# An adaLN block with segment-memory attention: the opening rearranged (modulation on TensorE, key and query blocks interleaved, weight splits in another place)

## The chip, the cores and the metric

The kernel runs on one core of one Trainium2 chip. The metric is the time of one execution on the device in microseconds; a kernel's time is the median of several runs. A profile is one execution, recorded by the hardware profiler; its times count from the start of the span.

## What is computed

One sequence of 2048 rows of 512 values (`x`) passes through an attention with a compressive memory and then through a gated bilinear network. A conditioning vector `c` gives six vectors of 512 (shift, scale and gate for each half) through one matrix. Cut to what matters here:

```python
mod = (silu(c) @ w_mod).reshape(1, 6, 1, 512)
sa, ca, ga, sb, cb, gb = (mod[:, i] for i in range(6))

h = layernorm(x) * (1 + ca) + sa
q, k, v = h @ wq, h @ wk, h @ wv          # 32 heads of 16, 4 segments of 512 rows
for s in range(4):
    p = softmax(q_s k_s^T / 4 + causal)
    a_mem = (phi(q_s) M) / (phi(q_s) z + 1e-6)     # phi(t) = t + 1 if t > 0 else exp(t)
    o_s = g * a_mem + (1 - g) * (p v_s)            # g = sigmoid(beta), per head
    M, z = M + phi(k_s)^T v_s, z + sum(phi(k_s))
x = x + ga * (o @ wo)
h = layernorm(x) * (1 + cb) + sb
x = x + gb * (((h @ w_gate) * (h @ w_up)) @ w_down)
```

Everything is float32. The projections are done as three products of split operands: each operand is written as a high part, rounded for TensorE's fast float32 form, and a low part, the rest; high times high, low times high and high times low are added up.

## The kernel before, in words

**Stages.** The sequence is cut into four segments of 512 rows, and the heads into four groups of eight. For one segment the normalised rows are transposed into four tiles of 128 columns (`h`, split into `ahH` and `ahL`), and each group's keys and queries come from twelve matmuls per block (`a_kq`: four column tiles, three products each). Keys and queries are written to DRAM in three bfloat16 parts (`kd`, `qd`) and read back in another layout (`kst`, `qst`) by `load`. Then a loop over 32 units (a segment, a group, half of its heads) does the scores twice: once for the row maxima (`q_step`, tiles `q`, reduced on VectorE into `nm`), once for the exponentials (`k_step`, tiles `k` and `pt`), and then the product with the values (`av_step`, tile `tb`). What the next segments need (projections, layer norm, memory) is fed in between as filling. The last part of the program is the network (`acc`, `X`, `Y`, `Z`).

**The opening**, which is where the change is, runs ahead of that loop, for segment 0. Its parts are:

- the silu of `c` (`s_c`), and the gates from `beta` (`gg`, `omg`, `hmg` and one column of each value tile `v`)
- 20 warm-up matmuls on zeros (`warm`, tile `wups`) while the first loads are under way
- the modulation for the first layer norm, in two halves of 256 columns of shift and scale each (`mod0(0)`, `mod0(1)`, weights `wm`, result `m`, then `mod0_out` into `modc`). The first half is 16 one-column products on TensorE with warm-up matmuls between; the second is summed on VectorE, scaled by `s_c`, and reduced by TensorE with a column of ones
- the layer norm `ln`: statistics, reciprocal root, normalising four tiles of `x`, 16 transposes into four banks (`atp`, one bank for each column tile), and for each column tile shift and scale on ScalarE (`ahf`), high part and low part on VectorE
- the weight splits: `load_g(nm, w, g)` loads the keys' or queries' weights of one group (`wrk`, `wrq`), makes the high part on ScalarE (`wkH`, `wqH`) and the low part on VectorE or GpSimd (`wkL`, `wqL`). `load_v` does the same for the value weights
- `a_kq(0, 0, ...)`, `a_v(0)` (tile `vps`), `a_kq(0, 1, ...)`, with parts of the scores of unit 0 between.

**What sets the order.** TensorE's order is written out: every matmul and transpose is chained to the one before by the helpers `MM` and `TP` (lines 85 and 88). `CV` and `CA` are such chains for VectorE and ScalarE (both record line 39), so what is called through them stays in the order of the program. What is called through `vec`, `act` or `nc.gpsimd` is placed by a scheduler that has its own model of times, within the data's dependences; `pin` only ties a place to TensorE's last instruction. All loads and stores here are issued from SP's queue, in the order that the scheduler gave them. The buffers of the raw weights are taken from a list of tags (`stage`), so that group 1's and group 2's raw weights lie where the four tiles of `x` lay, and their loads wait until these are transposed. The gating of the chip's TensorE clock is outside of the program; the profile tells it as a granted share.

The driver of the opening in the kernel before reads, in short:

```python
next(lng); next(lng)      # statistics, normalising
mod0(0)
next(lng); next(lng)      # column tiles 0 and 1
mod0(1)
hcur[0] = run(lng)        # column tiles 2 and 3
```

## Time and profile before

| | us |
|---|---|
| median of 3 runs | 870.56 |
| lowest and highest | 870.12, 871.88 |
| the profiled execution | 869.22 |
| its span | 867.5 |
| TensorE busy in the span | 840.5 |
| VectorE busy | 649.4 |
| ScalarE busy | 495.9 |
| GpSimd busy | 276.3 |

Busy times of engines overlap, so they don't add up to the span. The granted TensorE clock has a mean of 0.998 over the span. A row of a timeline gives start, length (of the whole run, where several alike are merged), engine, line, operation, output and inputs, shape, and in brackets the idle time just before it with what ended it. The pages call the weight load PEld and the matmul PE; a float32 product is two instructions of each. A matmul's length includes its way through the array, and the next one starts before it ends, so the cost of one in a row is the distance of the starts.

### The profile page before, as it was taken

The page shows a single profiled execution, that of the slowest core. Times are in us where ns is not written, and L with a number is a line of the kernel's source. Part 1 is how long each engine was busy: PE and PEld are TensorE (multiplying, and loading weights), DVE is VectorE, ACT ScalarE, POOL GpSimd, SP SyncE. Part 2 cuts the span into 40 slices and gives each one's busy share as a digit, 9 for nine tenths or more (in the row PEclk, how much of TensorE's full clock was granted, in tenths as well). Part 3 has the DMA queues.
Part 4 walks back from the last instruction along what each step waited for, and adds up shares of the span by engine and source line. Part 5 has one row for each costly group of instructions (what it writes and reads, how often), then busy time and mean ns, then how long its engine had stood idle before and what let it go on. Part 6 is the DMA issues. An engine that isn't in the chain of part 4 may idle for free.

```text
span 867.5 us, 14401 instructions
## 1 busy us (share of the span) xinstructions
PE 840.5 (97%) x4969; PEld 598.1 (69%) x4970; DVE 649.4 (75%) x1802; ACT 495.9 (57%) x757; POOL 276.3 (32%) x424
## 2 busy tenths in 40 slices
PE   8989999999999999999999999999999999999998
PEld 5755656565665566665666677788888778888886
DVE  8698766887778877778879457989987855446654
ACT  3758757677777686677544626344536546365230
POOL 4545536466546574586424620000000000000000
PEclk9999999999999999999999999999999999999999
DMA  7555443546436444547476348559561575435002
GB/s 235 160 165 133 128 108 102 174 128 178 125 97 178 129 129 134 135 144 235 133 234 181 124 160 269 203 199 339 204 239 49 187 264 213 161 134 182 28 22 97
DMA packets 83928, 139.57 MB, mean 161 GB/s; under 512 B 12720, under 2 KB 46768, under 8 KB 83856
## 3 DMA queue, kind: packets, MB, share of 16 engines
q1 hardware_dynamic: 83568, 138.52, 50.7%
q8 instruction: 39, 0.64, 0.3%
q14 instruction: 33, 0.27, 0.1%
q10 hardware_dynamic: 288, 0.15, 0.1%
HBM read 89.87 MB, written 48.50 MB: 160 GB/s over the span
## 4 chain that ended last, share of the span: by engine, by line
PE 81%; DVE 12%; ACT 5%; issue 1%; DMA 0%; DVEq 0%; ACTq 0%
PE acc L1337 14%; PE tb L85 8%; PE Xu L1268 7%; PE Xg L1268 7%; PE k L85 6%; PE q L85 6%; DVE q L39 6%; PE vps L85 5%; PE wops L85 5%; PE Yu L1268 4%; PE Yg L1268 4%; PE qps L85 3%; PE kps L85 3%; ACT pt L324 2%; PE Zg L1268 1%; PE Zu L1268 1%
## 5 line engine op out<-in xcount | busy, mean ns | idle before, releaser
L39 DVE CUSTOM_DVE_ANT_0 q<-q,cmask 128x384 f32<-128x384 f32 (+3 forms) x512 | 245.7, 508 | 61.0 <-PE q L85 53.1
L324 ACT ACTIVATE pt<-k 128x1024 f32<-128x1024 f32 x160 | 163.9, 1024 | 65.0 <-PE k L85 64.5
L330 POOL TENSOR_SCALAR_AFFINE_SELECT pt<-pt 128x256 f32<-128x256 f32 (+1 forms) x224 | 98.0, 452 | 165.0 <-ACT pt L324 164.6
L85 PE MATMUL q<-kst,qst 96*128 96x384 bf16 (+3 forms) x512 | 103.1, 298 | 12.5 <-DVE nm L39 11.2
L85 PE MATMUL k<-qst,kst 98*128 98x384 bf16 (+3 forms) x512 | 97.1, 302 | 4.4 <-ACT pt L324 4.2
L1345 DVE TENSOR_TENSOR xa<-xa,acc 128x512 f32<-128x512 f32 x95 | 64.7, 683 | 39.9 <-PE acc L1337 39.4
L85 PE MATMUL tb<-pt,v 128*32 128x512 f32 (+3 forms) x1024 | 75.5, 436 | 0.0
L39 DVE DVE_READ_ACCUMULATOR2_ANT nm<- 128x1 f32 x512 | 71.8, 140 | 0.0
L85 PEld LDWEIGHTS <-kst 98*128 98x128 bf16 x512 | 37.7, 98 | 48.8 <-issue 42.8
L85 PEld LDWEIGHTS <-qst 96*128 96x128 bf16 x512 | 45.6, 97 | 34.9 <-issue 12.5
L1337 PE MATMUL acc<-dH,mH 128*128 128x512 f32 (+1 forms) x152 | 60.3, 397 | 0.0
L1337 PE MATMUL acc<-dL,mH 128*128 128x512 f32 (+1 forms) x152 | 60.1, 395 | 0.0
L1337 PE MATMUL acc<-dH,mL 128*128 128x512 f32 (+1 forms) x152 | 60.0, 395 | 0.0
L85 PEld LDWEIGHTS tb<-pt,v 128*32 128x32 f32 x1024 | 28.7, 109 | 38.6 <-issue 34.8
L356 ACT ACTIVATE tsb<-tb 128x512 f32<-128x512 f32 x32 | 19.1, 596 | 40.2 <-PE tb L85 40.2
L1337 PEld LDWEIGHTS acc<-dL,mH 128*128 128x128 f32 (+1 forms) x152 | 28.6, 188 | 7.1
L1337 PEld LDWEIGHTS acc<-dH,mL 128*128 128x128 f32 (+1 forms) x152 | 28.5, 188 | 7.1 <-DVE mL L1288 0.3
L1337 PEld LDWEIGHTS acc<-dH,mH 128*128 128x128 f32 (+1 forms) x152 | 28.5, 188 | 6.7
L85 PE MATMUL kps<-ahH,wkH 128*128 128x512 f32 x64 | 29.9, 466 | 0.0
L85 PE MATMUL wops<-woH,oH 128*128 128x512 f32 x64 | 28.2, 440 | 0.7 <-ACT oH L519 0.7
L85 PE MATMUL qps<-ahH,wqH 128*128 128x512 f32 x64 | 28.7, 448 | 0.0
L85 PE MATMUL vps<-wvH,ahH 128*128 128x512 f32 x64 | 28.3, 442 | 0.0
(400 smaller groups left out, 2031.3 us busy)
## 6 DMA issues: line engine op xcount, KB each, us to landing
wm<-in_w_mod_dram SPq DMA_DIRECT2D x24, 256.0 KB, 4.5
kd<-k SPq DMA_DIRECT2D x16, 384.0 KB, 2.5
kst<-kd SPq DMA_DIRECT2D x32, 192.0 KB, 3.2
qd<-q SPq DMA_DIRECT2D x16, 384.0 KB, 2.8
qst<-qd SPq DMA_DIRECT2D x32, 192.0 KB, 3.6
x<-in_x_dram SPq DMA_DIRECT2D x16, 256.0 KB, 4.5
kst<-kd SPq DMA_DIRECT2D x32, 128.0 KB, 3.1
qst<-qd SPq DMA_DIRECT2D x32, 128.0 KB, 3.5
```

Of the source, the lines that this page charges most:

```text
L39: i = getattr(self.eng, name)(*a, **k)
L85: return pe(nc.tensor.matmul(*a, **k))
L324: ex = act.activation(pt, kp, AF.Exp, scale=0.25)
L330: sels[u, i] = nc.gpsimd.affine_select(w, w, pattern=[[0, w.shape[1]], [1, P]], compare_op=ALU.is_ge, fill=0.0, base=0, channel_multiplier=-1)
L356: act.activation(tsbs[u], tbs.pop(u), AF.Copy)
L1268: pe(nc.tensor.matmul(ps[0:n], a, b[:, k], start=first and c == 0, stop=last and c == 5, skip_group_check=True))
L1337: pe(nc.tensor.matmul(ps, a[0:m, t * P:(t + 1) * P], b[0:m], start=j == 0, stop=j == n - 1))
L1345: vec.tensor_add(xa, xa, ps)
```

## The change

Nothing behind the opening is edited. The order of instructions differs on every engine, up to the first scores on TensorE and to the loads of segment 1's `x` on SP. The core of the diff:

```diff
-            eng.tensor_scalar(b, mv[:, :, 1], 1.0, EPS, op0=ALU.mult, op1=ALU.add)
-            eng.tensor_mul(b, b, a)
+        if first:
+            CV.scalar_tensor_tensor(b, mv[:, :, 1], EPS, a, op0=ALU.add, op1=ALU.mult)
...
+        tps = [bank(f"{pfx}tp{s}_{d}") for d in range(KT)] if first else []
         for t in range(4):
             i = V.tensor_scalar(xt[t], xt[t], mv[:, t, 0:1], y[:, t:t + 1],
...
+            for d, ps in enumerate(tps):
+                TP(ps[:, t * P:(t + 1) * P], xt[t][:, d * P:(d + 1) * P], ident)
...
             if fast:
-                V.tensor_copy(hi, h)
+                if d % 2:
+                    A.activation(hi, h, AF.Copy)
+                else:
+                    V.tensor_copy(hi, h)
                 V.tensor_sub(lo, h, hi.bitcast(F32))
...
-    for a in kst:
-        nc.gpsimd.memset(a[96:98].rearrange("p h t -> p (h t)").bitcast(F32), ONES2)
...
+    scl = CV.tensor_mul(s_c, s_c, e1)
+    for a in kst:
+        tc.add_manual_dep(nc.gpsimd.memset(a[96:98].rearrange("p h t -> p (h t)").bitcast(F32), ONES2).ins, scl.ins.name, SYNC, reason="order")
...
+    def gates():
...
+    MW = 96
...
     def mod0(j):
-        ps = mp0[j][:, 0:4]
-        if j == 0:
+        ps = mp0[j].rearrange("p (i n) -> p i n", n=P)[:, :, 0:MW]
+        for k in range(KT):
             for i in range(4):
-                for k in range(KT):
-                    MM(ps[:, i:i + 1], r0[0][k][:, i * P:(i + 1) * P], s_c[:, k:k + 1],
-                       start=k == 0, stop=k == KT - 1)
-                    if i == 0:
-                        warm(2)
-                if 0 < i < 3:
-                    warm(2)
-            a0 = r0[1][0]
-            CV.tensor_scalar_mul(a0, a0, s_c[:, 0:1])
-            for k in range(1, KT):
-                CV.scalar_tensor_tensor(a0, r0[1][k], s_c[:, k:k + 1], a0, op0=ALU.mult, op1=ALU.add)
...
+                MM(ps[:, i], r0[j][k][:, i * P:(i + 1) * P], s_c[:, k:k + 1].to_broadcast([P, MW]),
+                   start=k == i == 0, stop=k == KT - 1, skip_group_check=True)
...
-        A, V = (CA if g == 0 else act), (CV if g == 0 and nm == "q" else nc.gpsimd)
+        A, V = CA if g < 2 else act, CV if g == 0 else nc.gpsimd
...
+            three = ((wH, hH), (wH, hL), (wL, hH)) if s == 0 and g < 2 else ((wH, hH), (wL, hH), (wH, hL))
+            terms = [(k, *ab) for k in range(KT) for ab in three]
+            if s == 0 and g == 1:
+                terms.sort(key=lambda t: t[1] is wL)
...
-                        i = act.activation(a, f, fn)
+                        i = (CA if fast else act).activation(a, f, fn)
...
-    next(lng)
     mod0(0)
     next(lng)
+    mod0_out(0, mp0[0])
+    mod0(1)
+    next(lw[0])
     next(lng)
-    mod0(1)
-    hcur[0] = run(lng)
+    next(lng)
+    mod0_out(1, mp0[1])
     next(lw[1])
...
     kq0 = [a_kq(0, 0, "k"), a_kq(0, 0, "q")]
+    for kq in kq0:
+        next(kq)
+        next(kq)
+    run(lng)
+    for _ in range(4):
+        next(lw[2])
...
+    gates()
```

`gates()` holds what was written out before at the place of the silu: the two exponentials of `beta`, the sums and reciprocals, the copies into the value tiles and the products into `hmg`. It is called behind the splits of group 1.

What that makes of the order shows at two places. The first is TensorE from the modulation to the first key block. `wm_0` to `wm_3` are the modulation weights of the four row tiles of `w_mod`, `x_0` to `x_3` the four tiles of rows, and `atp_0` to `atp_3` the four column tiles. Before, from the end of the first half on (the second transposes and the key block follow):

```order
L85 MATMUL m_272<-s_c,wm_2_239 128x1
L85 MATMUL m_272<-s_c,wm_3_240 128x1
L88 MATMUL atp_0_366<-ident,x_0_206 128x128
L88 MATMUL atp_0_366<-ident,x_1_208 128x128
L88 MATMUL atp_0_366<-ident,x_2_210 128x128
L88 MATMUL atp_0_366<-ident,x_3_212 128x128
L88 MATMUL atp_1_377<-ident,x_0_206 128x128
L88 MATMUL atp_1_377<-ident,x_1_208 128x128
L88 MATMUL atp_1_377<-ident,x_2_210 128x128
L88 MATMUL atp_1_377<-ident,x_3_212 128x128
L85 MATMUL m_273<-ones,wm_0_237 128x1 x4
L88 MATMUL atp_2_394<-ident,x_0_206 128x128
```

All four transposes of a column tile stand together, eight of them ahead of the second half's reduction and eight behind it. Now, from the end of the last transposes on:

```order
L88 MATMUL atp_2_321<-ident,x_3_208 128x128
L88 MATMUL atp_3_322<-ident,x_3_208 128x128
L85 MATMUL m_251<-s_c,wm_0_233 128x96 x4
L85 MATMUL m_251<-s_c,wm_1_234 128x96 x4
L85 MATMUL m_251<-s_c,wm_2_235 128x96 x4
L85 MATMUL m_251<-s_c,wm_3_236 128x96 x4
L85 MATMUL kps_0_379<-ahH_0_365,wkH_253 128x512
L85 MATMUL kps_0_379<-ahL_0_366,wkH_253 128x512
L85 MATMUL kps_0_379<-ahH_0_365,wkL_254 128x512
```

The second half is done on TensorE as 16 products behind all 16 transposes, which go tile by tile of `x`; the first key and query blocks follow and take turns by column tile (0 and 1 of the keys, 0 and 1 of the queries, then 2 and 3 of each).

The second place is ScalarE from the value weights to the splits of group 1 (`wkH` and `wqH` in the last rows of each). Before:

```order
L39 ACTIVATE wvH_286<-wrv_288 128x512
L39 ACTIVATE wvH_290<-wrv_292 128x512
L39 ACTIVATE kf_0_435<-kps_0_422 128x512
L39 ACTIVATE k_0_0_437<-kf_0_435 128x512
L39 ACTIVATE wvH_294<-wrv_296 128x512
L39 ACTIVATE wvH_298<-wrv_300 128x512
L842 ACTIVATE rlk_0_479<-kf_0_435 128x512
L842 ACTIVATE phk_0_478<-kf_0_435 128x512
L39 ACTIVATE qf_0_469<-qps_0_456 128x512
L39 ACTIVATE q_0_0_471<-qf_0_469 128x512
L761 ACTIVATE wkH_449<-wrk_448 128x4x8x16
L761 ACTIVATE wqH_453<-wrq_452 128x4x8x16
```

Now:

```order
L39 ACTIVATE wvH_272<-wrv_274 128x512
L39 ACTIVATE wvH_276<-wrv_278 128x512
L39 ACTIVATE kf_0_422<-kps_0_379 128x512
L39 ACTIVATE k_0_0_424<-kf_0_422 128x512
L39 ACTIVATE qf_0_442<-qps_0_386 128x512
L39 ACTIVATE q_0_0_444<-qf_0_442 128x512
L39 ACTIVATE rlk_0_452<-kf_0_422 128x512
L39 ACTIVATE phk_0_451<-kf_0_422 128x512
L39 ACTIVATE wkH_432<-wrk_431 128x4x8x16
L39 ACTIVATE wqH_436<-wrq_435 128x4x8x16
L39 ACTIVATE gg<-be 128x32
```

All four value weights stand ahead of the keys' evacuation, the queries' follows the keys' at once, ahead of the features, and the splits of group 1 are chained behind them (line 39 in place of 761). On GpSimd their low parts now stand ahead of the gates' copies, and the low part of group 0's key weights has gone to VectorE, between the two writes of `modc`.

More of the change, by code (lines that the diff above doesn't have):

```diff
@@ L147, in tile_kernel @@
     hm8 = cst.tile([P, HG], F32, name="hm8")
-    vec.tensor_reduce(hm8, ident.rearrange("p (d h) -> p h d", h=HG), axis=AX.X, op=ALU.add)
+    CV.tensor_reduce(hm8, ident.rearrange("p (d h) -> p h d", h=HG), axis=AX.X, op=ALU.add)
     for g in range(NG):
-        vec.tensor_copy(hmg[:, g], hm8.unsqueeze(2).to_broadcast([P, HG, VS]))
+        CV.tensor_copy(hmg[:, g], hm8.unsqueeze(2).to_broadcast([P, HG, VS]))
     modc = cst.tile([P, 16], F32, name="modc")
@@ L206, in ln @@
         hH, hL = [], []
+        if first:
+            hcur[0] = hH, hL
         for d in range(KT):
-            ps = bank(f"{pfx}tp{s}_{d}", small=pfx == "c" and s == 0)
-            for t in range(4):
-                TP(ps[:, t * P:(t + 1) * P], xt[t][:, d * P:(d + 1) * P], ident)
+            if first:
+                ps = tps[d]
+            else:
+                ps = bank(f"{pfx}tp{s}_{d}", small=pfx == "c" and s == 0)
+                for t in range(4):
+                    TP(ps[:, t * P:(t + 1) * P], xt[t][:, d * P:(d + 1) * P], ident)
             h = pool.tile([P, L], F32, tag="hf", name=f"{pfx}hf{s}_{d}", bufs=hb[2])
@@ L846, in feature2 @@
                 def feature2():
-                    pin(vec.scalar_tensor_tensor(e, e, 1.0, rl, op0=ALU.min, op1=ALU.add))
+                    pin((CV if fast else vec).scalar_tensor_tensor(e, e, 1.0, rl, op0=ALU.min, op1=ALU.add))
                 held = s == 0 and g > 1
```

58 lines of the change are left out of this document (25 added, 33 removed).

## The prediction

> **What bounds the kernel now.** I read the page's shares first, then the chain of waits over the first 90 us, then each engine's timeline of that stretch, since the order of the instructions differs nowhere behind about 50 us.
>
> ```profile
> PE 840.5 (97%) x4969; PEld 598.1 (69%) x4970; DVE 649.4 (75%) x1802; ACT 495.9 (57%) x757; POOL 276.3 (32%) x424
> PE 81%; DVE 12%; ACT 5%; issue 1%; DMA 0%; DVEq 0%; ACTq 0%
> ```
>
> TensorE is busy for 97% of the span and holds 81% of the chain that ended last. So an opening that ends earlier brings the rest forward as a block, unless something behind it is tied to another clock. What the opening waits for stands in the chain (start, length, what):
>
> ```profile
> 10.82 1.91 DVE x L39 x4
> 12.74 1.68 DVE wm L39
> ...
> 16.11 0.67 DVE wm L39
> ...
> 16.83 1.20 PE m L85 x8
> 18.02 1.40 PE atp L88 x6
> ...
> 26.51 5.58 PE vps L85 x24
> ...
> 39.76 0.51 PE q L85 x2
> ```
>
> Until 16.8 us VectorE decides: it normalises `x`, then sums the second half of the modulation weights (`wm`) by itself, four passes over 512 columns. TensorE waits for that sum, reduces it (`m`), does the second eight transposes (`atp`), and from there is bound by itself up to the first scores (`q`). TensorE's timeline gives its prices:
>
> ```profile
> 8.79 0.28 PE L85 MATMUL m<-s_c,wm 128*128 128x1 f32 x2
> 13.66 0.95 PE L85 MATMUL m<-s_c,wm 128*128 128x1 f32 x8
> 14.46 1.07 PE L88 MATMUL atp<-ident,x 128*128 128x128 f32 x8
> 16.83 1.20 PE L85 MATMUL m<-ones,wm 128*128 128x1 f32 x8 [1.29 <-DVE wm L39]
> 17.89 1.95 PE L88 MATMUL atp<-ident,x 128*128 128x128 f32 x8
> 26.35 0.39 PE L85 MATMUL vps<-wvH,ahH 128*128 128x512 f32 x1
> 39.68 0.59 PE L85 MATMUL q<-kst,qst 96*128 96x512 bf16 x2
> 50.04 1.09 PE L85 MATMUL mz<-v,pkr 128*128 128x136 f32 x8
> ```
>
> A 512-column matmul of the projections costs 5.58/24 = 0.232 us, by the chain's piece at 26.51. Eight transposes cost (1.07 − 0.27)/7 = 0.114 us each at full clock, their own duration of 0.27 taken off. The second eight need nearly twice that, and the granted clock (second value from the right of the last four) tells why:
>
> ```profile
> 16.00:17.00 1.00, 0.17 (x2) 0.18 (x2) 0.77 (x3) 0.79 (x2) 0.00 (x0) 1.00 1.02 377
> 17.00:18.00 1.00, 1.00 (x9) 1.00 (x10) 0.94 (x2) 0.66 (x1) 0.00 (x0) 0.79 0.16 57
> 20.00:21.00 1.00, 1.00 (x4) 0.75 (x3) 0.67 (x2) 1.00 (x3) 0.00 (x0) 0.50 0.40 118
> 21.00:22.00 1.00, 1.00 (x6) 0.82 (x5) 0.97 (x3) 1.00 (x2) 0.00 (x0) 1.00 1.10 332
> ```
>
> The clock falls to 0.50 at about 17.6 us, after the 1.29 us wait, and is back at 21.0. So the wait costs twice: itself, and half the speed for 3.4 us.
>
> **The change part by part.** *Modulation on TensorE.* Removed: four VectorE passes, eight one-column reductions, twelve warm-up matmuls among the first half's products. Added: both halves as 16 products each, 96 columns wide, which are 32 instructions a half (two per float32 product, as in the x2 and x8 of the rows). No row shows this shape. Below stands the one-column product, 0.114 us (0.95 less a duration of 0.15 or so, over 7); above, if load and product did not overlap, the 0.23 of 512 columns. The nearest row is `mz`, float32 with 136 columns: (1.09 − 0.28)/7 = 0.116. I take 0.116, so 3.71 us a half. TensorE comes free for the first at 8.79 as before. Its line is then:
>
> - first half 8.79 + 3.71 = 12.50
> - sixteen transposes × 0.114 = 1.83, to 14.33
> - second half 3.71, to 18.04
> - 24 matmuls of the first key and query blocks × 0.232 = 5.57, to 23.61.
>
> The values' matmuls begin at 23.61 where they began at 26.35: 2.74 us earlier, provided that nothing else is late. Each supplier in turn:
>
> The data of the second half: its last load is issued by 8.56 us and lands at most 6.2 later, at 14.8; its product is due at 14.33 + 2.78 = 17.1.
>
> ```profile
> 6.12 2.44 SPq L654 DMA_DIRECT2D wm<-in_w_mod_dram  x4
> DMA to landing us min/median/max: 5.0/5.9/6.2
> ```
>
> The normalised `x`: even at its old time (10.82, done at 12.73) the four tiles arrive at 11.3, 11.8, 12.3 and 12.73, and transposes that take one tile after the other ask for them at 12.50, 12.96, 13.4 and 13.9. So the layer norm's shorter arithmetic, the gates moved behind and the memsets of `kst` moved behind the silu gain nothing by themselves. The memsets could cost:
>
> ```profile
> 1.77 3.97 POOL L248 MEMSET kst<- 2x1024 f32 x4
> 7.60 1.49 POOL L672 TENSOR_TENSOR hmg<-hmg,gg 128x128 f32<-128x128 f32 x4
> 29.10 1.94 POOL L762 TENSOR_TENSOR wkL<-wrk,wkH 128x512 fp32r<-128x512 f32 x1 [14.98 <-ACT wkH L761]
> 30.98 2.12 POOL L762 TENSOR_TENSOR wqL<-wrq,wqH 128x512 fp32r<-128x512 f32 x1
> ```
>
> VectorE's and ScalarE's prices, for this and for what follows, are
>
> ```profile
> 8.44 0.66 DVE L39 BATCH_NORM_STATS2 ast<-x 128x6 f32<-128x512 f32 x1
> 20.30 0.43 DVE L39 CAST ahH<-ahf 128x512 fp32r<-128x512 f32 x1 [0.93 <-ACT ahf L39]
> 20.76 0.69 DVE L39 TENSOR_TENSOR ahL<-ahf,ahH 128x512 fp32r<-128x512 f32 x1
> 22.44 1.20 DVE L39 TENSOR_TENSOR wqL<-wrq,wqH 128x512 fp32r<-128x512 f32 x1
> 29.52 2.06 DVE L39 TENSOR_TENSOR q<-qr,q 128x512 bf16<-128x512 f32 x1
> ```
>
> ```profile
> 19.49 1.45 ACT L39 ACTIVATE ahf<-atp,modc 128x512 f32<-128x512 f32 x2 [1.83 <-PE atp L88]
> 21.83 1.19 ACT L39 ACTIVATE wvH<-wrv 128x512 fp32r<-128x512 f32 x2
> 23.25 0.60 ACT L39 ACTIVATE kf<-kps 128x512 f32<-128x512 f32 x1 [0.23 <-PE kps L85]
> 27.79 1.23 ACT L761 ACTIVATE wkH<-wrk 128x512 fp32r<-128x512 f32 x1
> ```
>
> The memsets' 3.97 us now lie behind the silu, some 3 to 7 us in, beside the layer norm's statistics. If they held these back to 7.3, four statistics of about 0.8 us would end at 10.5, where they ended at 9.3 (8.44 + 0.66 + their last small step): the last tile would come at about 13.9, just when its transposes are due. If not, nothing is late either. The statistic at 8.44 kept its 0.66 beside GpSimd's `hmg` at 7.60, so I take nothing.
>
> Columns 0 and 1 of `h` wait for the transposes at 14.3, not for the second half, and are split by about 17, before TensorE turns to them at 18.04: the keys' low weights, now on VectorE (1.2 us at about 12.9), lie in time that VectorE has free. Columns 2 and 3 wait for the second half: scales by 18.5, `wqL` by 19.7, `ahL_2` by 20.84, and with ScalarE's copy of column 3 at 20.55, `ahL_3` by 21.45. TensorE asks for them at 19.9, 21.06 and 22.45. The cover is the twelve matmuls of columns 0 and 1 for both blocks, 2.8 us; it is enough by only 0.2 us, so a little may be lost. Without it (keys first, then queries, as before) TensorE would stand for some 1.2 us.
>
> *The queries' parts.* The subtraction at 29.52 took 2.06 us instead of 0.69: it ended only when GpSimd was between `wkL` and `wqL`. Now ScalarE does the four value weights, `kf`, `k`, `qf`, `q`, two features and only then `wkH`, at about 26.5. VectorE, released from 24.35 on, does three steps each for keys and queries (0.69 + 0.43 + 0.69, with gaps 1.85 us) and ends at about 28.0; GpSimd starts group 1 at 27.7. The queries' store is issued at 28.0, not 31.65:
>
> ```profile
> 31.65 0.38 SPq L824 DMA_DIRECT2D qd<-q  x1
> 35.58 2.62 SPq L262 DMA_DIRECT2D qst<-qd  x6
> qd<-q SPq DMA_DIRECT2D x2, 384.0 KB, 3.4
> qst<-qd SPq DMA_DIRECT2D x3, 192.0 KB, 3.5
> ```
>
> Store 3.4, then three loads issued within 0.9 us, 3.5 each to landing: 35.9. On SP's queue the two stores now stand behind four weight loads, whose buffers the transposes free by 14.3, and the queries' loads behind four of the keys', which wait for the keys' store (issued at 26.2, landed by 29.6) and are issued by 31.4: neither holds them. TensorE reaches the first scores 13.33 us (39.68 − 26.35) after the values began, at 36.94. So the queries land 1.0 us early, and TensorE sets the start again.
>
> *Low weights last in group 1.* TensorE comes to group 1's keys at 23.61 + 24 × 0.232 = 29.2. GpSimd has `wkL` at 29.6 and `wqL` at 31.7, by the rows above. In the old order the second matmul would wait; in the new one they are due at 31.0 and 33.9. This keeps the 2.74 and adds nothing. Behind them GpSimd now does the gates' copies, late by some 3 us and wanted only for the first memory product near 47 us: nothing. Group 1's stores (now with group 3's weight loads and a load of `x` ahead of them on SP) stay near 41.6 and 43, as GpSimd is busy for longer; their loads come only at about 50: nothing.
>
> The sum: −2.74, with 0.2 either way. The profiled execution took 869.22 us (867.5 of span and 1.72 around it), hence 866.5. The median of the runs shown is 1.34 us above it, hence **867.8**.
>
> **The rivals.**
>
> - *The clock falls once more.* Warm-up matmuls are gone and a run of transposes stands between the halves. For: such a fall is in the rows above, after one-column products, eight transposes and a pause. Against: 96 columns keep the array streaming and TensorE no longer pauses. One stretch of 3.4 us at 0.50 costs 1.7 us: 869.5. The Trainium skill ("TensorE: Matmul & The Clock Gate", Part 4) speaks for this rival: transposes, it says, do not count as work for the clock, and the sum by that rule would be this 869.5. Its Part 1 speaks against it, asking for a whole idle stretch of about 3.4 us before the clock falls. The trace does not bear Part 1 out, as 1.29 us of waiting were enough.
> - *The clock falls for longer, which is the slower side.* The point is whether a stretch with narrow float32 products alone keeps the clock; no row shows one without 512-column matmuls. If not, it halves from about 14.2: the second half takes 7.4 us to 21.7, the clock comes back at about 24.4, six of the 24 matmuls run at 0.46, the rest at 0.232, to 28.6. That is 2.25 later than 26.35: 870.56 + 2.25 = 872.8.
> - *The queries are late.* If GpSimd takes `wkL` just before the queries' last subtraction, it waits 1.9 us, the 1.0 of slack goes, and 0.9 of the gain with it; traffic can add one more: 868.7 to 869.7.
> - *The gain does not carry.* Between 48 and 66 us the scores wait for VectorE. If something there holds its old time (GpSimd's later chain, the second group's stores), nothing is left: 870.5. Against: VectorE's first piece there is the scores themselves.
>
> **How the numbers follow.** Forecast 0.70, one fall of the clock 0.09, the long fall 0.08, late queries 0.07, lost later 0.06. A run of this kernel is told from no change by about 0.2%, 1.74 us: faster is below 868.8, slower above 872.3. Faster: 0.70 and a little of the late queries, 0.72. Slower: the long fall and some unknown, 0.09. The rest, 0.19, is within. The range goes from 866.4 (1.4 us more, as an execution whose clock rises sooner ends the warm-up sooner, and the runs' own spread allow) to 870.7, which takes in all rivals but the long fall.
>
> **What would show it.** Right: the products `m` 128x96 at 0.11 to 0.12 us apart, clock 1.00 from about 7.4 on, the values' first matmul near 23.6, the first scores near 36.9, the queries' store issued near 28. Wrong: any 0.50 in the clock's rows behind 8 us, `m` over 0.13 apart, a wait of the scores for `qst`, or scores 2.7 us earlier and an end that is not.

## The result, and the profile after

| | before | changed |
|---|---|---|
| median, us (7 executions each) | 870.56 | 867.61 |
| lowest and highest | 869.48, 872.57 | 866.65, 867.79 |
| the profiled execution | 869.22 | 867.63 |
| its span | 867.5 | 865.9 |

The ratio is 0.9963 with an interval of 0.9951 to 0.9974: faster by 0.37%. The changed kernel was timed again beside the last experiments (label changed_again) and gave 866.97 (866.64 to 866.99, 5 executions) against 871.12, ratio 0.9950 [0.9936, 0.9964]. Its twelve executions together have a median of 867.1.

The page of the changed kernel, engine shares and the chain of waits by engine:

```profile
PE 840.0 (97%) x4982; PEld 598.4 (69%) x4982; DVE 648.3 (75%) x1796; ACT 496.4 (57%) x759; POOL 273.9 (32%) x423
PE 80%; DVE 11%; ACT 6%; POOL 1%; issue 1%; DMA 1%; DVEq 0%; POOLq 0%; ACTq 0%
```

Nothing here tells the two kernels apart; the opening's chain does (start, length, what), again of the changed kernel:

```profile
9.03 3.54 PE m L85 x32
12.57 1.75 PE atp L88 x16
14.32 3.55 PE m L85 x32
17.86 1.42 PE kps L85 x6
...
23.47 5.58 PE vps L85 x24
29.05 1.80 PE kps L85 x8
30.84 1.02 ACT wqH L764
...
34.25 3.74 DVE phk L853
37.99 0.61 DVE q L39
```

VectorE's normalising and summing are gone from the front: from the first product on, TensorE is the chain by itself up to 30.8 us. What is new stands at the end of the piece: one VectorE sum, `phk` of group 1, lasting 3.74 us, with the first score reduction behind it. The starts in TensorE's timeline of the changed kernel:

```profile
8.86 3.71 PE L85 MATMUL m<-s_c,wm 128*128 128x96 f32 x32
12.41 1.91 PE L88 MATMUL atp<-ident,x 128*128 128x128 f32 x16
14.15 3.71 PE L85 MATMUL m<-s_c,wm 128*128 128x96 f32 x32
17.65 0.48 PE L85 MATMUL kps<-ahH,wkH 128*128 128x512 f32 x1
23.31 0.39 PE L85 MATMUL vps<-wvH,ahH 128*128 128x512 f32 x1
36.56 0.61 PE L85 MATMUL q<-kst,qst 96*128 96x512 bf16 x2
```

The values begin at 23.31 (26.35 before), the first scores at 36.56 (39.68): 3.04 and 3.12 us earlier. The table by stretches gives, for each stretch, the busy time of TensorE, its weight loads, VectorE, ScalarE and GpSimd, each with the number of instructions, then the granted clock, the DMA share and GB/s. The clock (third value from the end) is at 1.00 where it had 0.79 and 0.50:

```profile
17.00:18.00 1.00, 1.00 (x10) 0.96 (x10) 0.10 (x2) 0.17 (x1) 0.00 (x0) 1.00 1.13 318
20.00:21.00 1.00, 1.00 (x6) 0.78 (x6) 0.92 (x3) 1.00 (x3) 0.00 (x0) 1.00 0.62 154
```

SP's queue issues the queries' store at 27.84 (31.65 before):

```profile
27.84 0.37 SPq L830 DMA_DIRECT2D qd<-q  x1
30.81 1.23 SPq L274 DMA_DIRECT2D qst<-qd  x3
```

Of 3.12 us at the first scores, the two profiled executions keep 1.57 at the end. The piece that is lost right behind the scores can be seen on VectorE and GpSimd. First VectorE's timeline, then GpSimd's, of the changed kernel:

```profile
34.25 3.74 DVE L853 SCALAR_TENSOR_TENSOR phk<-phk,rlk 128x512 f32<-128x512 f32 x1 [1.02 <-ACT phk L848]
37.91 0.69 DVE L39 CUSTOM_DVE_ANT_0 q<-q,cmask 128x512 f32<-128x512 f32 x1
```

```profile
34.22 1.68 POOL L765 TENSOR_TENSOR wkL<-wrk,wkH 128x512 fp32r<-128x512 f32 x1
35.83 1.62 POOL L765 TENSOR_TENSOR wqL<-wrq,wqH 128x512 fp32r<-128x512 f32 x1
37.40 1.14 POOL L691 TENSOR_TENSOR hmg<-hmg,omg 128x8 f32<-128x8 f32 x4
```

The sum takes 0.69 us where GpSimd is idle. Here GpSimd began `wkL` 0.03 us ahead of it and took `wqL` next. By its end at 37.99 and its own 0.69 us, VectorE got through only at about 37.3. The first reduction starts 1.35 us after the first scores. In the second profile of the same kernel (changed_again) the very same sum got in between `wkL` and `wqL`, took 2.16 us, and the reduction came 0.43 us after the scores at 36.30. Its lines, VectorE and then GpSimd:

```profile
34.00 2.16 DVE L853 SCALAR_TENSOR_TENSOR phk<-phk,rlk 128x512 f32<-128x512 f32 x1 [1.01 <-ACT phk L848]
36.73 0.70 DVE L39 CUSTOM_DVE_ANT_0 q<-q,cmask 128x512 f32<-128x512 f32 x1 [0.57 <-PE q L85]
```

```profile
33.97 1.65 POOL L765 TENSOR_TENSOR wkL<-wrk,wkH 128x512 fp32r<-128x512 f32 x1
35.57 2.09 POOL L765 TENSOR_TENSOR wqL<-wrq,wqH 128x512 fp32r<-128x512 f32 x1
```

What this costs shows when TensorE's instructions are set beside those of the kernel before, one by one. The changed kernel's profile is 3.12 us ahead at the first scores and 2.58 at about 52 us: 0.54 is lost. In changed_again, where the sum got in early, it is 3.37 and 3.30 at the same two instructions. The profiles of the experiments below fall into the same two groups. Where the first reduction starts 1.2 to 1.5 us after the first scores (changed, e1, e4, e6, e11, e12), 0.42 to 0.65 us of the lead is lost by 52 us; where it starts 0.43 us after them (changed_again, e3, e5, e8, e9), less than 0.1.

Behind 52 us the lead goes down in three steps, near 198 us (to 2.34), 383 us (to 1.91) and 825 us (to 1.57).

- The first belongs to the change. It is there, with 0.20 to 0.22 us, in all eleven profiles of kernels whose gates come late, and in neither e2 nor e8, whose gates come early. GpSimd's `mem` near 188 us then waits for ScalarE's `q` and not for `qf`, what GpSimd does next runs on beside VectorE's normalising of a later tile of `x`, and this takes 0.75 us instead of 0.55. Why the wait is another one is not known.
- The second belongs rather to the one profile of before: e2 and e8, which gain nothing in the opening, lose 0.49 and 0.44 us against it at the same place.
- The third, and others of 0.1 to 0.3 us near 533 us, differ between executions of one program: changed_again falls behind by 0.25 us at 533 us against the first profile and gains as much at 826.

### The profile page after: what moved, and what is told of

Read it like the earlier page. It is cut to its first block, busy times and chain, and to the rows that moved or that the text cites. A ratio compares the mean times of both kernels' runs of the same rounds, so it can differ in the third digit from the quotient of the medians.

```text
span 865.9 us, 14418 instructions
## 1 busy us (share of the span) xinstructions
PE 840.0 (97%) x4982; PEld 598.4 (69%) x4982; DVE 648.3 (75%) x1796; ACT 496.4 (57%) x759; POOL 273.9 (32%) x423
## 4 chain that ended last, share of the span: by engine, by line
PE 80%; DVE 11%; ACT 6%; POOL 1%; issue 1%; DMA 1%; DVEq 0%; POOLq 0%; ACTq 0%
PE acc L1350 14%; PE tb L85 7%; PE Xg L1281 7%; PE Xu L1281 7%; PE k L85 6%; DVE q L39 6%; PE q L85 5%; PE vps L85 5%; PE wops L85 5%; PE Yu L1281 4%; PE Yg L1281 4%; PE kps L85 3%; PE qps L85 3%; ACT pt L336 2%; PE Zg L1281 1%; PE Zu L1281 1%
```

## The experiments

Each runs against the kernel before on the same chip. Times are medians.

| label | us | lowest, highest | executions | ratio to before |
|---|---|---|---|---|
| e1_half2_dve | 867.55 | 866.81, 868.03 | 4 | 0.9962 [0.9947, 0.9977] |
| e2_mod_alone | 870.65 | 869.5, 872.55 | 10 | 1.0001 [0.9991, 1.0011] |
| e3_blocks_in_turn | 867.97 | 867.39, 868.66 | 7 | 0.9967 [0.9956, 0.9979] |
| e4_splits_free | 870.19 | 868.72, 870.92 | 10 | 0.9988 [0.9979, 0.9998] |
| e5_low_in_place | 866.81 | 866.55, 867.45 | 4 | 0.9949 [0.9932, 0.9965] |
| e6_warm16 | 866.49 | 866.28, 866.71 | 4 | 0.9944 [0.9928, 0.9960] |
| e8_gates_early | 871.52 | 869.8, 872.47 | 10 | 1.0005 [0.9994, 1.0015] |
| e9_one_column | 869.34 | 868.18, 875.21 | 10 | 0.9994 [0.9973, 1.0014] |
| changed_again | 866.97 | 866.64, 866.99 | 5 | 0.9950 [0.9936, 0.9964] |
| e11_memset_early | 866.81 | 866.61, 867.71 | 5 | 0.9952 [0.9939, 0.9964] |
| e12_warm16_low_in_place | 867.03 | 866.35, 867.08 | 5 | 0.9950 [0.9937, 0.9962] |
| e13_and_phi1_late | 872.16 | 867.07, 873.9 | 11 | 1.0010 [0.9997, 1.0023] |

The changed kernel itself, once more, as the yardstick:

> The changed kernel, word for word, on the chip and beside the runs of the kernel before that the three other variants of this set share. Nothing separates the theories here: 867 to 868 us, ratio 0.996 to 0.997. It is the yardstick for the two variants that may be faster than it: a difference under 0.4 us from it counts as none.

It came at 866.97, and five of the variants lie within 0.6 us of it.

### Is it the sum on VectorE?

**e1: the changed kernel with the second half summed on VectorE again.**

```diff
     def mod0(j):
+        if j == 1:
+            CV.tensor_scalar_mul(a0, a0, s_c[:, 0:1])
+            for k in range(1, KT):
+                CV.scalar_tensor_tensor(a0, r0[1][k], s_c[:, k:k + 1], a0, op0=ALU.mult, op1=ALU.add)
...
+            for i in range(4):
+                MM(ps[:, i, 0:1], a0[:, i * P:(i + 1) * P], ones[:, 0:1], start=True, stop=True)
+            return
```

> The changed kernel with the second half of the modulation summed on VectorE again (four passes, then four one-column products), at its place behind the transposes; all else as changed. Two theories. A, the wait for that sum is what the change removed: TensorE waits again and the values' matmuls begin at about 26, as before (23.3 in the changed kernel). B, the sum is no longer late since the layer norm ends 0.9 us sooner and GpSimd's split no longer lies beside it, and what counts is the clock: the sum ends at about 15.3, the products at 16.3, the split parts let the first key matmuls begin at about 17; the values begin at 23.4 to 23.6 if the clock holds, at about 25.2 if TensorE's pause of some 1 us at 14.3 makes it fall for 3.4 us.

The time is the changed kernel's, 867.55. TensorE's timeline shows that the wait for the sum is there again, 1.21 us, though behind sixteen transposes and not eight:

```profile
15.39 1.05 PE L85 MATMUL m<-ones,wm 128*128 128x1 f32 x8 [1.21 <-DVE wm L39]
24.44 0.39 PE L85 MATMUL vps<-wvH,ahH 128*128 128x512 f32 x1
```

From the first product to the values it takes 15.72 us, in the changed kernel 14.45: the clock was at 0.50 from 17.43 to 20.84. Three of its four executions have a mean granted clock of 0.997 or 0.998, at 867.29 to 868.03; the one that kept it, at 1.000, took 866.81. That is theory B. Beside the one execution that kept the clock, the fall costs 0.5 to 1.2 us, and that one is as fast as the changed kernel. So with the layer norm earlier, moving the sum is not what carries the gain.

**e2: the kernel before with the modulation alone on TensorE**, 96 columns wide; the order of everything else is left.

```diff
+    MW = 96
...
+        for k in range(KT):
             for i in range(4):
+                MM(ps[:, i], r0[j][k][:, i * P:(i + 1) * P], s_c[:, k:k + 1].to_broadcast([P, MW]),
+                   start=k == i == 0, stop=k == KT - 1, skip_group_check=True)
+        mod0_out(j, mp0[j])
```

> The kernel before with both modulation halves as 96-column products on TensorE, nothing else changed. If the modulation is the whole gain, the values begin at 23.3 to 23.7 and the time falls by about 3 us. If the other parts are needed: TensorE is through with the second half at about 17.3 and the transposes at 18.2, waits for the split parts of columns 2 and 3 and for the queries' low weights (about 22.1), and the values begin at about 24.7, 1.6 us sooner than before; the queries' last subtraction still stands beside GpSimd's splits, so that the first scores come at 38.5 to 39.5 and the time falls by 0.3 to 1.2 us. The clock stays at 1.00 behind 8 us.

It gains nothing: 1.0001. I had expected up to 1.2 us. TensorE's wait moves from the sum to the layer norm; these are VectorE's line and TensorE's, then the row of the stretch behind:

```profile
11.49 3.12 DVE L39 TENSOR_SCALAR x<-x,amv,ay 128x512 f32<-128x512 f32 x4
```

```profile
14.66 0.83 PE L88 MATMUL atp<-ident,x 128*128 128x128 f32 x5 [1.33 <-DVE x L39]
15.28 5.32 PE L85 MATMUL m<-s_c,wm 128*128 128x96 f32 x32
```

```profile
15.23:18.64 3.41, 3.41 (x18) 3.41 (x17) 2.15 (x4) 1.24 (x2) 0.00 (x0) 0.50 0.61 223
```

Normalising took 3.12 us instead of 1.91, since group 0's `wkL` came on GpSimd beside it (12.58 to 14.33); TensorE stood for 1.33 us, the clock fell, and the second half's products ran at half speed up to 18.64 us. The profiled execution is one of four with a mean clock of 0.997 or 0.998, at 871.80 to 872.55 us; the six with 0.999 or 1.000 took 869.50 to 871.17. The kernel before with such a clock took 869.55 to 871.05 on that chip, so the modulation alone gains nothing even where the clock stays up.

### The order around it

**e8: the changed kernel with the gates where they are defined**, ahead of the layer norm in VectorE's written order.

```diff
+    gates()
+
     def mod_acc(r):
...
-    gates()
     w2 = [load_g(nm, w, 2) for nm, w in (("k", wk_), ("q", wq))]
```

> The changed kernel with the gates' arithmetic at its old place ahead of the layer norm. Theory: of the 3.1 us that the first scores gain, 0.5 is lost at once because VectorE's subtraction phk of group 1 (34.25, 3.74 us) waits until GpSimd is through with group 2's low weights and the gates' products, and the first reduction of scores behind it comes at 37.9 instead of 37.2. With the gates early GpSimd is through about 3.9 us sooner: phk ends by 36.6, the reduction begins with the scores, and the row maxima's store (nt) stands 0.4 to 0.5 us nearer to the first scores than in the changed kernel (12.24 us there); the layer norm ends 0.3 to 0.9 us later and moves nothing. Rival: the wait on phk is hidden by the order of TensorE and nt stays 12.2 behind the scores.

All of the gain is gone: 871.52, where I had expected a later layer norm to move nothing. VectorE's timeline, GpSimd's, and TensorE's show the mechanism:

```profile
10.08 0.35 DVE L39 RECIPROCAL omg<-omg 128x32 f32<-128x32 f32 x1 [3.67 <-POOL v L684]
10.35 0.64 DVE L39 BATCH_NORM_STATS2 ast<-x 128x6 f32<-128x512 f32 x1
```

```profile
5.02 3.68 POOL L676 MEMSET kst<- 2x1024 f32 x4 [2.75 <-DVE s_c L39]
8.77 1.28 POOL L684 COPY v<-omg 128x32 f32<-128x32 f32 x8
```

```profile
15.67 3.29 PE L88 MATMUL atp<-ident,x 128*128 128x128 f32 x16 [3.57 <-DVE x L39]
```

The reciprocal works in place on `omg`, which GpSimd has yet to copy into the value tiles, and these copies stand behind the four memsets. VectorE waits 3.67 us with the layer norm's statistics queued behind; they start at 10.35 instead of 5.21. TensorE waits 3.57 us for `x`, and the clock falls at 15.04 for 3.42 us. Values at 27.97. The theory's own point did come: `phk` takes 1.01 us at 38.92, and the first reduction starts 0.43 us after the scores; it is far too small to count here.

So the loss is that of the gates ahead of the layer norm while the memsets stand ahead of the gates' copies. In the kernel before, with both at their old places, the copies began at 6.38 us and the statistics at 6.08. The changed order with both at their old places was not run.

**e11: the memsets at their old place**, the gates still far behind.

```diff
     kst = [ap.tile([98, HQ, L], BF, name=f"kst{i}") for i in range(NB)]
+    for a in kst:
+        nc.gpsimd.memset(a[96:98].rearrange("p h t -> p (h t)").bitcast(F32), ONES2)
...
     scl = CV.tensor_mul(s_c, s_c, e1)
-    for a in kst:
-        tc.add_manual_dep(nc.gpsimd.memset(...).ins, scl.ins.name, SYNC, reason="order")
```

> The changed kernel with the four memsets of kst at their old place, the program's opening, instead of behind silu(c). Theory (the prediction's words, that their move gains nothing by itself): as long as the gates are far behind, nothing waits for GpSimd before group 1's first low weights at about 27.5 us, so values within 0.2 us of the same distance from the modulation's first product (14.45 us in the changed kernel's profile), time within 0.4 us of the changed kernel's. Rival (the memsets were moved because they hold up the layer norm's opening, either by slowing VectorE's statistics or by holding the mask's selection): the layer norm's x normalised 0.5 us or more later than in the changed kernel, values up to 0.5 us later, time 0.4 us or more above the changed kernel's.

866.81 beside 866.97: no difference. `x` is normalised from 9.93 us (9.97 in changed_again), the values come 14.52 us after the first product (14.46). With the gates behind, the memsets' place is worth nothing; in e8 it counts, because the gates wait behind them.

**e4: group 1's high parts where the scheduler puts them.**

```diff
-        A, V = CA if g < 2 else act, CV if g == 0 else nc.gpsimd
+        A, V = CA if g == 0 else act, CV if g == 0 else nc.gpsimd
```

> The changed kernel with group 1's high parts on ScalarE put where the scheduler wants them: they come ahead of the queries' copy. If the place of the splits carries the gain to the scores: GpSimd's low parts begin at about 26, VectorE's steps for the queries stand behind them, the queries' store is issued at 30 to 31.6 in place of 27.8, the first scores come at 38.4 to 39.6 in place of 36.6, and 1.8 us or more of the gain is lost. If there is slack enough, the scores move by less than 0.5 us.

870.19: most of the gain is lost; 0.8 us is left against the 871.0 of the kernel before on that chip. ScalarE's, SP's and TensorE's timelines:

```profile
23.89 1.19 ACT L764 ACTIVATE wkH<-wrk 128x512 fp32r<-128x512 f32 x1
24.85 1.28 ACT L764 ACTIVATE wqH<-wrq 128x512 fp32r<-128x512 f32 x1
25.89 0.66 ACT L39 ACTIVATE q<-qf 128x512 bf16<-128x512 f32 x1
```

```profile
30.11 0.37 SPq L830 DMA_DIRECT2D qd<-q  x1
```

```profile
38.50 0.60 PE L85 MATMUL q<-kst,qst 96*128 96x512 bf16 x2 [2.31 <-DMA qst<-qd]
```

The two high parts stand ahead of the queries' copy, GpSimd starts its low parts at 25.22 beside VectorE's three steps for the queries, the store is issued at 30.11, and TensorE waits 2.31 us for the queries. The values had begun at 22.74, 3.61 us ahead of before, among the earliest of all. At the first scores 1.18 us of that is left, and behind `phk`, which takes 6.41 us here, 0.53. An opening that ends early is worth little while this transfer is late.

**e3: key block whole, then query block.**

```diff
     kq0 = [a_kq(0, 0, "k"), a_kq(0, 0, "q")]
-    for kq in kq0:
-        next(kq)
-        next(kq)
     run(lng)
     for _ in range(4):
         next(lw[2])
-    for kq in kq0:
-        next(kq)
```

> The changed kernel with the first key block done whole and then the query block. If the turn by column tile is the cover that the prediction says, TensorE waits for ahH_2, ahL_2 and ahL_3 and the values begin 0.8 to 1.2 us later (24.1 to 24.5), and the first scores as much. If it is no cover, because the split parts come early enough, nothing moves (23.3).

From the first product to the values 15.70 us, 1.25 more than in turns: TensorE waits for `ahH_2` and `ahL_2`, and the starts slip by 0.49 and 0.50 us there. From the first product to the first scores it is 28.95 us, 27.70 in the changed kernel: the 1.25 is kept. (By the span's clock it is 0.73, because the first product itself began 0.52 earlier here.) The time, 867.97, is 0.8 above the twelve executions' median and 0.4 above the first seven's.

**e5: no sorting of the low weights.** 

```diff
-            if s == 0 and g == 1:
-                terms.sort(key=lambda t: t[1] is wL)
```

> The changed kernel with the low weights of group 1 not put last (high-high, high-low, low-high for each column tile). If the prediction is right that TensorE would wait for GpSimd there, group 1's keys stop for wkL and the scores come 0.2 to 0.5 us later. By the trace of the changed kernel wkL is ready at 29.3 us and would be asked for at 29.35, wqL at 31.5 and 32.1: then nothing moves, the scores stay 27.7 us behind the first modulation product and the time within 0.2 us.

866.81. `wkL` was there at 28.92 and the first product with it, the third of the block, began at 28.97: nothing waited, and the sorting gives nothing. This isn't the order of before, though, in which the low weights come second (high-high, low-high, high-low). That place is taken at 28.72 here, 0.20 us ahead of `wkL`; the old order was not run.

### The clock

**e9: the changed kernel with products one column wide.**

```diff
-    MW = 96
+    MW = 1
```

> The changed kernel with products of one column in place of 96 (same weights, same number, same output). A product costs the same by the rows of before (0.114 us, set by the weight load). If the clock goes by the streaming of columns, it falls to 0.50 within the products and the transposes (at about 11 to 14.5 or 17.7, by where its 3.4 us stretches lie), and the values begin at 24.9 to 28.5. If it goes by pauses, it stays at 1.00, the values begin at 23.3 and the width of 96 is worth nothing. If transposes do not count as work, the changed kernel itself is on the edge and this one falls early.

Each half takes as long as with 96 columns: the second starts at 14.09 and ends with the keys' start at 17.58, 3.49 us (changed kernel 3.50). TensorE never waits. Yet the clock falls. The table by stretches of this variant, cut where the clock changes:

```profile
10.81:14.23 3.42, 3.42 (x33) 3.42 (x33) 2.37 (x6) 1.41 (x2) 0.00 (x0) 1.00 1.12 341
14.23:17.64 3.41, 3.41 (x34) 3.41 (x32) 1.81 (x3) 2.83 (x4) 0.00 (x0) 1.00 1.06 364
17.64:21.05 3.41, 3.41 (x9) 2.68 (x9) 3.09 (x7) 2.94 (x5) 0.00 (x0) 0.50 1.01 256
```

and of the changed kernel, whose stretches lie within 0.1 us of these:

```profile
14.31:17.72 3.41, 3.41 (x34) 3.41 (x32) 1.81 (x3) 2.83 (x4) 0.00 (x0) 1.00 1.06 364
17.72:21.13 3.41, 3.41 (x17) 2.79 (x16) 3.11 (x7) 2.88 (x5) 0.00 (x0) 1.00 0.97 242
```

The middle rows agree in every count, 3.41 of 3.41 us busy and 34 matmuls; only the columns per matmul differ, and the stretch behind has 9 matmuls at 0.50 in one and 17 at 1.00 in the other. The values come 1.5 us later. It is no matter of one profile: all ten executions have a mean clock of 0.998 or less, and all twelve of the changed kernel 0.999 or 1.000. Two go down to 0.992 and 0.990 (874.57 and 875.21 us), four or five stretches' worth; where these lie is not known. So the width is worth about 2.2 us of the median against 867.1, 2.5 against e5 on the same chip, and much of the spread.

**e6: sixteen warm-ups instead of twenty, and e12: the same with e5's edit.**

```diff
-    NWU = 20
+    NWU = 16
```

> The changed kernel with 16 warm-up matmuls instead of 20. If TensorE sets the opening from its first instruction on, the first product begins when its weights land (8.1 us) instead of 8.9, and everything behind it, up to the row maxima's store, stands 0.7 to 0.8 us earlier than in the changed kernel's profile; in executions whose clock rises early the warm-up ends before the weights land anyway, so the median falls by 0.2 to 0.6 us. If another supplier is bound (layer norm, weights' splits), the values stay at 23.3. A pause ahead of the first product could make the clock fall; then the values come at 24 or later.

> Two parts of the changed kernel taken together that were each at least as fast by themselves (866.49 and 866.81 us): sixteen warm-up products instead of twenty, and group 1's low weights in their old place instead of last. Theory A (both were real: fewer warm-ups let the modulation start as soon as its weights land, about 0.5 us earlier, and the order of the low weights is worth nothing): 866.0 to 866.8 us, the modulation's first product at 8.2 to 8.4 us, 0.7 us or more under the changed kernel of this set. Theory B (the start of the modulation goes by when its weights land and by the phase of the clock, which differ from one execution to the next, and both medians came low because the chip of that set gave them so): within 0.4 us of the changed kernel of this set.

e6 looked 1.1 us faster than the changed kernel's first median, but e12, on one chip with changed_again, gives 867.03 beside 866.97. The time is theory B's. The start of theory A came too, 8.29 and 8.30 us, but it moves less than thought. TensorE waits for the weights and starts at 8.14 to 8.36 us wherever the warm-ups are through by then, with twenty of them too (e3, e5, e11); only where the clock rises late, at 6.9 us or later (changed, changed_again, e1, e9), do twenty hold it, to 8.59 to 8.86. No version here is shown to beat the changed kernel.

### The sum beside GpSimd

**e13: e12 with `phk` of group 1 behind the first two reductions.**

```diff
-                later.append(feature2)
+                (after_n if s == 0 and g == 1 else later).append(feature2)
```

> As the variant with sixteen warm-ups and the low weights in place, and group 1's VectorE sum phk behind the first two score reductions instead of ahead of them. In the changed kernel that sum took 3.74 us beside GpSimd's work (34.25 to 37.99 us) where 0.69 us is its length alone, and the first score reduction, queued behind it, started at 37.91 us, 1.35 us after the first scores. Theory C (what the changed kernel loses between the first scores, 3.12 us ahead of the kernel before, and 52 us, 2.58 us ahead, is that wait): the first score reduction starts within 0.9 us of the first scores, and the time is 0.3 to 0.6 us under the variant without this edit. Rival D (the sum is only stretched elsewhere, in the middle of the reductions, beside GpSimd's kr, qr, k and q, and the reductions behind it come late instead): nt at the same distance from the first scores as without the edit, time within 0.3 us of it or above.

872.16, 5.1 us more than e12. The first reduction did start 0.43 us after the scores, as C said; the rest is rival D, which had put no size to its "or above". VectorE's, GpSimd's (first and last of four in a row) and TensorE's lines, and the stretch behind:

```profile
37.78 4.69 DVE L39 SCALAR_TENSOR_TENSOR phk<-phk,rlk 128x512 f32<-128x512 f32 x1
```

```profile
37.35 1.22 POOL L823 TENSOR_TENSOR kr<-kf,k 128x512 f32<-128x512 f32 x1
...
40.70 1.22 POOL L827 TENSOR_TENSOR q<-qr,q 128x512 bf16<-128x512 f32 x1
```

```profile
43.45 0.38 PE L85 MATMUL q<-kst,qst 96*128 96x512 bf16 x1 [3.48 <-DVE nm L39]
```

```profile
44.06:47.47 3.41, 3.11 (x8) 2.11 (x8) 1.65 (x6) 0.60 (x1) 0.00 (x0) 0.50 1.04 327
```

The sum met GpSimd's `kr`, `qr`, `k` and `q`, four instructions with no gap, and ended 0.6 us after the last of them. TensorE stood 3.48 us for want of a reduced block, and the clock fell for 3.41 us on top, behind a stretch (40.65 to 44.06) in which TensorE was busy for 0.38 us. One of the eleven executions took 867.07, as e12 does; that fits a sum that got in early, but there is no profile of it.

## Why the prediction was right, and where its steps were not

The median, 867.61, is 0.2 us from the 867.8 of the text. The way to the first scores was as forecast; that the end came out so close is luck. Step by step:

**The line to the values held, its terms a little large.** A half of the modulation took 3.55 and 3.50 us instead of 3.71: an instruction of 96 columns costs 0.109 to 0.111 us, not the 0.116 of `mz` with its 136. The transposes took 1.74 (1.83), the two blocks 5.66 (5.57). With a start 0.07 later the sum is 23.31 instead of 23.61. No supplier was late: `x` was ready at 11.82, the interleaved blocks ran without a wait, and the cover that I had priced at 1.2 us was worth 1.25 in e3.

**The clock stayed at 1.00** from 7.49 us to 864.23, 1.7 us before the end of the span. The two rivals on it did not come, but e9 shows that the width is what kept them off. That "1.29 us of waiting were enough" for the fall of before, as the text has it, is not shown: in e9 the clock fell at the same distance from its rise, 10.24 us, without any wait. Nor does one fall show in the time of the kernel before: of its 56 executions beside the experiments, the 17 with a mean clock of 0.998, one stretch's worth, have a median of 870.13 us, the ten with 0.999 or 1.000 one of 870.18.

**The queries' parts, as said.** Store at 27.84 (28.0); the loads landed at 35.2 to 36.2 (35.9), and the scores did not wait. Two sizes were off and cancel: the store landed in 2.95 us (3.4), the loads took 4.4 to 4.6 (3.5). The slack was 0.4 us and not 1.0. e4 shows that this edit is a condition for the whole: without it a lead of 3.61 us at the values is 1.18 at the scores.

**"Hence 867.8" is right by two errors that cancel.** The text takes 2.74 us off the profiled execution (866.5) and adds the 1.34 by which that execution lay under its median. The changed kernel's profiled execution took 867.63, 1.1 more than that, and lies on its median.

*Too much gain.* The profiled executions differ by 1.59 us at the end, though the first scores came 3.12 earlier. So half of one of the text's own signs of being wrong came, "scores 2.7 us earlier and an end that is not", and with it a part of the rival "The gain does not carry". The step that failed is "an opening that ends earlier brings the rest forward as a block". 0.54 us went by 52 us with `phk` beside GpSimd's work, a term that is missing from my sum: the text looked for such a loss between 48 and 66 us, where it is under 0.1. The gates' copies and products (31.55 to 34.2 us) hold group 2's splits back to 34.2 to 37.4, where `phk` now comes; before, these ran from 33.91 to 37.2 and `phk` came at 37.25, behind them. Another 0.22 went near 198 us, also with the gates' place. The 0.4 near 383 us lies rather in the profile of before, and the 0.3 near 825 differs between executions: changed_again, without that and without the late `phk`, ends 2.22 us ahead.

*A wrong offset.* The profiled execution of the kernel before was a favourable one: at 869.22 it is under all 56 executions of that kernel beside the experiments, which have a median of 870.92. The granted clock goes with a part of that spread: the 28 with a mean of 0.996 or less, more than one stretch of 3.41 us at 0.50 (one is 3.41 × 0.5 / 867 = 0.002), have a median of 871.46, the 27 with 0.998 or more 870.13. All twelve executions of the changed kernel have 0.999 or 1.000, within 866.64 and 867.79. Still, most of the gain is there at an equal clock. The ten executions of before with 0.999 or 1.000, too much for a whole stretch at 0.50, took 869.55 to 871.05; their median is 3.1 us above the 867.1 of the twelve, where that of all 56 is 3.8 above. What else holds the ten back, and where in the program the second fall comes, is not known, as no such execution was profiled.

**"Gain nothing by themselves" left out what the moves do to each other.** I compared the old time of `x` with when the transposes ask for it and saw slack. What the gates would do inside the new order was not asked: VectorE's written order puts the layer norm behind a reciprocal, which waits for GpSimd's copies, which wait for the memsets. e8 puts the price of moving the memsets without the gates at 4.4 us, more than the whole gain. Of the memsets alone the sentence was right (e11). For gates and memsets both at their old places, which is the case that the old time of `x` stands for, it was not tested.

**"In the old order the second matmul would wait" fits the traces, by 0.2 us.** In the changed kernel `wkL` is ready at 29.31 and the second matmul of the block begins at 29.11. The sorting is not needed for that, as e5 shows: putting the low weights third is enough.

**What the gain comes from.** Removing the wait for VectorE's sum, which I put first, is neither enough (e2: 1.0001) nor needed (e1: 0.9962). What the gain does not survive is the loss of the layer norm's place ahead of the gates, with the memsets late (e8), of the queries' parts ahead of group 1's splits (e4) and of the clock that stays up (e9). Each undone alone gives back most or all of the gain, 4.4, 3.1 and 2.2 us by medians against 867.1, so their prices don't add up: whichever supplier is late sets the opening's end. Four parts were not undone by themselves: the transposes tile by tile of `x`, the layer norm's shorter arithmetic, ScalarE's high parts of columns 1 and 3, and the low part of group 0's key weights on VectorE. e2, where that low part on GpSimd stretched the normalising to 3.12 us, suggests that the last may count.

## What to carry to other kernels

In an opening where several chains end at nearly the same time, undo each part of a change by itself: the visible wait may be neither sufficient nor necessary, and an edit that moves nothing by the old profile can be what the rest stands on. Before an operation is placed on VectorE, above all one with two operands in memory, look at what GpSimd does at that time: a row of GpSimd instructions without a gap can hold it for the row's whole length, and which instructions queue behind it decides what that costs. And compare the one profiled execution, with its granted clock, to the other executions before its distance from their median is carried over to another kernel.

## What the runs showed of the hardware

**The clock goes by more than TensorE's idle time.** All changes of the clock inside the program lie on a grid of 3.41 us, whose phase differs from one execution to the next (the rise was at 4.3 to 7.5 us). The Trainium skill has this as a free-running window of 3413 ns ("TensorE: Matmul & The Clock Gate", Part 1, What's actually happening), and the runs agree. The Trainium skill has the clock fall after an idle window; here e9's stretch was busy for 3.41 of 3.41 us, by the profile's matmul lengths, and the clock fell, with one-column products; with 96 columns it stayed. Stretches that were busy for 2.12 us (before, 14.19 to 17.60) and 1.70 us (e1, 14.02 to 17.43) led to a fall too. In e9 the stretch before, one-column products and 16 transposes, kept the clock. Whether the transposes did this stays open: in all five profiles whose clock fell in the opening, the fall came 10.24 us, three stretches, after the rise, so that a least time at full clock would explain it as well.

**VectorE and GpSimd shut each other out for whole instructions, and VectorE can be passed over.** The sum `phk`, 0.69 us by itself, took 2.16, 3.74, 4.69 and 6.41 us beside GpSimd's two-operand instructions (changed_again, changed, e13, e4), and in the two profiles of one kernel it got in at different gaps. The Trainium skill says that whichever starts first has the ports that the two engines share for the whole instruction ("SBUF — State Buffer", Who interferes with whom). The lengths agree; that a waiting VectorE was passed over at the ends of three GpSimd instructions (e13), and in e4 of four, until GpSimd paused for 1.49 us at 39.53, goes beyond it. The layer norm's statistics, with one operand, kept their 0.66 to 0.69 us beside GpSimd's memsets (5.21 to 8.33 us in the changed kernel). The same section of the Trainium skill has it so for an instruction with at most one input in SBUF, the memory on the chip, outside VectorE's 2-port modes. One operand alone was no protection here: normalising `x` took 3.12 us instead of 1.91 beside `wkL` (e2), and the cast of the queries 1.77 instead of 0.43 beside `wqL` (e4).

**A float32 matmul instruction costs 0.109 to 0.111 us from 1 to 96 columns** at a clock of 1.00 (two of them make a product): 3.49 and 3.55 us for 32. Up to there the width cost nothing in time, and by e9 it bought the clock.
